# Two chained attentions and a hypernetwork MLP on one core: p loaded once, cast and turned at the start, and a new order of all steps

## The chip, the core and the metric

The kernel runs on one core of one Trainium2 chip. The metric is the device time of one execution in microseconds (us). Times inside the kernel are counted from the first instruction of the profiled execution. Engines are called as in the profile: PE (matmuls; PEld for its weight loads), DVE, ACT, POOL, and SP, which only issues DMAs.

## The reference

The inputs are q, k, v of 8 batches x 8 heads x 576 rows x 64, p of 8 x 8 x 32 x 64, and the matrices moe_w_q and moe_w_k (512 x 64) and moe_w_out (512 x 512), all fp32. The inputs are drawn at random, scaled by 0.1 and 1/sqrt(512).

```python
def sm_attn(qq, kk, vv):
    s = scale * np.matmul(qq, kk.transpose(0, 1, 3, 2))
    a = np.exp(s - np.max(s, axis=-1, keepdims=True))
    a = a / (np.sum(a, axis=-1, keepdims=True) + 1e-09)
    return np.matmul(a, vv)
p_packed = sm_attn(p, k, v)               # 32 rows for each head
x = sm_attn(q, p_packed, p_packed)        # 576 rows, heads side by side: 576 x 512
wq, wk = x @ w_q, x @ w_k                 # 576 x 64
mixed = np.einsum('bst,btd->bsd', scale * np.einsum('bsd,btd->bst', wq, wk), x)
out = np.maximum(mixed, 0.0) @ w_out      # 576 x 512, fp32
```

## The kernel before

The work goes batch by batch through one long sequence of steps; matmuls take bf16 and accumulate in fp32. Steps of neighbouring batches overlap. The order of all steps is written out by hand in one string, ORDER; each word is one step, and the program issues the steps of each engine's queue exactly in the order in which they stand there. The framework adds the waits between the engines. A word reads `NAME.batch.part@engine=banks`: V is DVE, A is ACT, P is POOL, S is SP; a word without an engine is a matmul step on PE, or a DMA; the banks are those of PSUM.

The steps of batch b are, in the order in which data flows:

- LD.k, LD.v, LD.q: the loads of k, v, q, on POOL's queue, cast from fp32 to bf16 by the DMA. Each tensor has four buffers. q0 and q7 come in two halves, LD.r (first half) and LD.q (second half). LD.H and LD.g are the two halves of k of batch 0: H as fp32 by SP, cast by HC on ACT, and g by POOL. Each load on POOL's queue waits, in that queue, for the landing of the eighth load before it.
- KT, QV: turns of k and q on DVE (32 x 32 transposes, L242). PX (one instruction) turns p for batches 2 to 7, EX the part of p for batches 0 and 1.
- S1 (L278 for batches 0 and 1, L288 for the others), X1: the scores of p against k, and their exponentials on ACT. For batches 0 and 1 (DIAG) p stands as block-diagonal copies in the tile pblk, which PB writes (one copy for each of the four quarters of the partitions); for the others the exponentials are turned by TE on DVE.
- PV (L321), RC, PP, PT: the product with v and, by a column of ones in v's tile, the sums; their reciprocal; the scaled p_packed; its turn.
- QK, QKE, QD: p_packed times the two small weights, their copies.
- S2 (L379), X2 (L384), RS (L400), RR (L405), AM (L411), AT (L420, L425), AE: the scores of q, exponentials, sums, reciprocals, the normalized weights (on DVE or POOL), their transposes on PE and the copies out of PSUM. Parts 0, 1, 2 are 256, 256 and 64 (of 128) rows; part 3 is 0 and 1 together, part 4 all.
- WKQ (L447, L452), WE, GM (L473), GE, Y, YE, MX (L498), MR, RL, RLR: the hypernetwork, down to the rectified mixed rows.
- OT (L546; OH for halves), OE, OEF, ST, STF, STH: the output matmul, the copy out of PSUM and the store. HOLD.v7 is a tiny DMA on SP's queue that waits for v of batch 7; the stores behind it on that queue can't start before.
- WARM (L621): matmuls on a tile of zeros whose result nobody reads. WARM.6 has 6 units of 128 columns. They stand where PE's queue is to be kept busy.
- SET: constants (masks, zeros, the column of ones, the identity).

p comes in three ways in the kernel before: E0 and E1, batches 0 and 1 in fp32 by ACT's and SP's queues, cast by EC, turned by EX and copied to pblk by PB; and four casting loads P0 to P3 on POOL's queue, one for each quarter of the partitions, of all batches, turned by PX.

Of the kernel before, what the change touches and what calls it, by code (L numbers as in the profile page):

```python
# [654 lines left out]
```

## Time and profile before

| what | value |
|---|---|
| median of three runs | 106.0 us (105.98 to 106.29) |
| the profiled execution's own time | 105.18 us |
| its span, first to last instruction | 103.3 us |
| granted PE clock, mean over the span | 0.991 |
| PE busy | 96.8 us (94%) |
| DVE, ACT, POOL busy | 75.7, 66.2, 49.9 us |
| moved by DMA | 25.16 MB counted at the landing, mean 244 GB/s |
| read from HBM, written to it | 30.28 MB, 9.44 MB |

Most loads cast fp32 to bf16, so they read twice the bytes that they land; GB/s in the profile counts the landed bytes. A busy PE in the profile includes the WARM steps. A row of the chain gives start, length and what the chain ran through; the chain is the path of work and waits that ended last.

### The profile page before, as it was taken

Reading aid. Unit: us, or ns where it says so; the run is one execution under the profiler, and the core shown is the slowest. Engines: PE = TensorE matmul, PEld = TensorE weight load, DVE = VectorE, ACT = ScalarE, POOL = GpSimd, SP = SyncE. Lnnn points to the kernel's source line nnn. Section 1 sums busy time; section 2 is a strip of 40 time slices with the busy share of each in tenths; the row PEclk is TensorE's granted clock in tenths of the full one; section 3 lists DMA queues with packets and bytes.
Section 4 is the critical chain, followed back from the end, with each engine's and each line's share of the span. In section 5 each row is a group of like instructions: output and inputs, shape, how many; then the busy total and the mean of one; then the engine's idle time right before and its main releaser. Section 6 shows DMA issues by size and latency. Waiting matters only on the chain.

```text
span 103.3 us, 3603 instructions
## 1 busy us (share of the span) xinstructions
PE 96.8 (94%) x1544; PEld 58.4 (57%) x1544; DVE 75.7 (73%) x150; ACT 66.2 (64%) x109; POOL 49.9 (48%) x76
## 2 busy tenths in 40 slices
...
PEclk9999999999999999999999999999999999999996
DMA  2999999999999999999999999999999999999884
GB/s 71 262 149 191 209 208 198 210 211 213 204 213 212 203 208 213 212 206 211 211 210 208 220 208 203 215 211 207 209 259 377 402 410 400 403 409 366 341 305 164
DMA packets 14079, 25.16 MB, mean 244 GB/s; under 512 B 2160, under 2 KB 7024, under 8 KB 14064
## 3 DMA queue, kind: packets, MB, share of 16 engines
...
q1 hardware_dynamic: 3200, 7.87, 19.9%
...
HBM read 30.28 MB, written 9.44 MB: 384 GB/s over the span
## 4 chain that ended last, share of the span: by engine, by line
PE 73%; DVE 9%; DMA 5%; ACT 5%; POOL 3%; issue 2%; DVEq 0%; POOLq 0%; ACTq 0%
PE ps L546 25%; PE ps L621 13%; PE ps L321 6%; DMA k_sb<-in_k_dram 5%; PE ps L379 5%; PE ps L452 4%; PE ps L498 4%; PE ps L425 4%; DVE rs L400 3%; ACT e L384 3%; PE ps L447 3%; PE ps L278 2%; PE ps L473 2%; PE ps L288 2%; PE ps L342 2%; POOL a L411 2%
## 5 line engine op out<-in xcount | busy, mean ns | idle before, releaser
L546 PE MATMUL ps<-wout,relu 128*128 128x512 bf16 x124 | 30.5, 380 | 0.0
L411 POOL TENSOR_TENSOR a<-e,rr 128x1024 bf16<-128x1024 f32 (+2 forms) x13 | 15.6, 1211 | 19.1 <-DVE rr L405 11.0
L621 PE MATMUL ps<-o 128*128 128x128 f32 (+3 forms) x76 | 23.6, 452 | 1.3 <-DVE o L134 1.2
L127 ACT ACTIVATE o<-ps 128x1024 f32<-128x1024 f32 (+2 forms) x17 | 15.0, 888 | 6.9 <-PE ps L546 6.3
L546 PEld LDWEIGHTS <-relu 128*128 128x128 bf16 x124 | 10.7, 98 | 12.3 <-issue 1.8
L621 PEld LDWEIGHTS ps<-o 128*128 128x128 f32 x76 | 12.7, 220 | 7.1 <-issue 4.9
L384 ACT ACTIVATE e<-ps 128x256 f32<-128x256 f32 (+2 forms) x19 | 11.3, 621 | 5.9 <-PE ps L379 5.5
L509 ACT ACTIVATE relu<-ps 128x1024 bf16<-128x1024 f32 (+1 forms) x14 | 12.7, 933 | 2.2 <-PE ps L498 1.1
L242 DVE STREAM_TRANSPOSE kT<-k_sb 128x1152 uint32<-128x1152 uint32 (+1 forms) x9 | 11.1, 1232 | 3.0 <-DMA k_sb<-in_k_dram 2.9
L176 POOL DMA_DIRECT2D v_sb<-in_v_dram x16 | 10.1, 637 | 6.4 <-PE ps L425 2.1
L242 DVE STREAM_TRANSPOSE qT<-q_sb 128x1152 uint32<-128x1152 uint32 (+1 forms) x10 | 11.2, 1119 | 0.7 <-DMA q_sb<-in_q_dram 0.7
L400 DVE TENSOR_REDUCE rs<-e 128x16 f32<-128x512 f32 (+2 forms) x13 | 10.9, 846 | 0.5 <-ACT e L384 0.4
L321 PE MATMUL ps<-v_sb,e 64*64 64x192 bf16 x288 | 7.5, 245 | 0.7 <-DVE o L131 0.7
L299 ACT ACTIVATE e1T<-ps 128x576 bf16<-128x576 f32 x12 | 7.2, 663 | 1.3 <-PE ps L288 1.2
L127 ACT ACTIVATE aT<-ps 128x128 bf16<-128x128 f32 (+2 forms) x11 | 5.3, 506 | 3.6 <-PE ps L425 2.1
L321 PEld LDWEIGHTS <-e 64*64 64x64 bf16 x288 | 6.0, 107 | 2.6 <-issue 0.9
L127 ACT ACTIVATE wkq<-ps 128x448 bf16<-128x448 f32 (+1 forms) x9 | 6.3, 713 | 1.7 <-PE ps L452 1.4
L452 PE MATMUL ps<-aT,pqk 128*128 128x256 bf16 (+1 forms) x48 | 6.8, 246 | 0.1
L379 PEld LDWEIGHTS <-qT 64*128 64x128 bf16 x320 | 5.5, 94 | 2.3 <-issue 0.7
L379 PE MATMUL ps<-ppT,qT 64*128 64x64 bf16 x320 | 6.6, 190 | 0.0
L179 POOL DMA_DIRECT2D k_sb<-in_k_dram x7 | 5.2, 745 | 2.7 <-ACT g L127 2.7
L447 PE MATMUL ps<-pqk,aT 128*128 128x64 bf16 x80 | 6.1, 194 | 0.1
...
## 6 DMA issues: line engine op xcount, KB each, us to landing
...
```

The costliest lines, as they stand in the source:

```text
L127: nc.scalar.activation(o, i, COPY)
L176: nc.gpsimd.dma_start(v_bufs[b % NL][halves(i), 0:7:2], src)
L242: nc.vector.transpose(o, i)
L321: nc.tensor.matmul(T["pv", b][halves(cc), i], lhsT, rhs, start=n == 0, stop=n == R - 1, skip_group_check=True)
L379: nc.tensor.matmul(ps[:, y, t - t0, i], lhsT, rhs, start=e == 0, stop=e == 1)
L384: nc.scalar.activation(e2[:, t0:t1].rearrange("a t (i y n) -> a y (t i) n", i=2, y=2), T["s2", b, c].rearrange("a y t i n -> a y (t i) n") ...
L400: nc.vector.tensor_reduce(rs[:, t0 * H:t1 * H], src, axis=AX, op=ADD)
L411: e.tensor_tensor(a2[:, t0:t1].rearrange("a t i (u l) -> a (t i u) l", l=L), e2v(b, c), T["rr", b][:, t0 * H:t1 * H].to_broadcast((P, (t1 ...
L452: nc.tensor.matmul(o, pqk[:, i, Dl:], aT[:, i, c0:c1], start=i == 0, stop=i == 1)
L509: nc.scalar.activation(o, i, RELU)
L546: nc.tensor.matmul(ps, lhsT, wout[:, j, :], start=j == 0, stop=j == NJ - 1)
L621: nc.tensor.matmul(bank(int(bk), [w]), warm[:, 0:P], rhs, start=True, stop=True)
```

## The change

p is loaded by one DMA on ACT's queue (LD.N), in fp32, for all batches. NC casts it in two halves, one on ACT and one on DVE; PX turns it in two halves on DVE, at the start. PB copies the block-diagonal parts for batches 0 and 1 from the turned p, two on DVE and two on ACT. LD.E0, LD.E1, LD.P0 to LD.P3, EC and EX are gone. The whole ORDER is new, with the same steps of the batches otherwise: 48 steps are on another engine than before (AM of batches 0 and 1, of part 2 of batch 2 and QD of several batches move to POOL; AM.6.3 moves to DVE; the others change mainly between DVE and ACT), the loads stand in another order towards the end (r7 is last, behind two stores on POOL's queue), and the WARM steps after S1.0 have 46 units instead of 62, those before it 21 instead of 20.

```diff
-SET.warm@V SET.v3@V SET.pz0@V LD.E0@A SET.tab@A SET.aT1@V LD.H@S LD.P3 LD.E1@S EC@A EX@V PB.0.1@V LD.g0
-SET.v0@P HC@A PB.0.3@V PB.0.2@V KT.0.0@V KT.0.1@V LD.v0 PB.0.0@P WARM.4=0 WARM.16.128=0 S1.0=0,1,2 X1.0.0@A WARM.6=3
-PV.0.0=4,5 PV.0.1 RC.0@V LD.q0 SET.mask@P SET.idf@V SET.aT0@V QV.0.1@V PP.0.0@V LD.P2 LD.r0 PP.0.1@V PT.0@V
-SET.v2@V LD.W0 QV.0.0@V WARM.15=3 S2.0.2=6,7 LD.k1 LD.W1 SET.aT2@V LD.P1 KT.1.2@V S2.0.1=0,1 X2.0.1@A RS.0.1@V
-SET.v1@P S2.0.0=2,3 X2.0.0@A LD.v1 LD.P0 WARM.8=4 QK.0=4 RR.0.1@V AM.0.1@V QKE.0@A LD.q1 RS.0.0@V SET.aff@P
-SET.idb@V WARM.3=5 S1.1=0,1,2 X1.1.0@A WARM.6=5 PV.1.0=4,5 PV.1.1 X2.0.2@A RR.0.0@V AT.0.1=3 AM.0.0@V AT.0.0=2
-AE.0.0@A RC.1@V PP.1.1@V RS.0.2@V RR.0.2@V AM.0.2@V AE.0.1@A QD.0@A WARM.5=0 WKQ.0.0=0,1 AT.0.2=5 LD.k2
-AE.0.2@A WARM.1=6 WKQ.0.2 LD.v2 WE.0.0@A WKQ.0.1 LD.q2 LD.k3 WE.0.1@A WARM.3=6 GM.0=5 PP.1.0@V PT.1@V QK.1=4
-QV.1.2@V S2.1.1=6,7 GE.0@A S2.1.0=2,3 LD.O PX@V S2.1.2=0,1 KT.2.2@V QKE.1@A X2.1.1@A RS.1.1@V X2.1.0@A Y.0=4,5
-YE.0@A WARM.1=6 S1.2=6,7,2,3 X2.1.2@A LD.v3 RS.1.0@V MX.0.1=4,5 RR.1.1@V X1.2.0@A TE.2.0@V X1.2.1@A TE.2.1@V
-RR.1.0@V WARM.7=0 PV.2.0=0,1 PV.2.1 RL.0.1@A RS.1.2@V AM.1.0@V QD.1@A MR.0=6,7 RLR.0@A LD.k4 RR.1.2@V
-MX.0.0=2,3 LD.q3 RC.2@V AT.1.0=4 AM.1.2@V AT.1.2=5 AE.1.2@A RL.0.0@A PP.2.1@V AM.1.1@P AT.1.1=6 AE.1.1@A
-PP.2.0@V AE.1.0@V WARM.2=7 WKQ.1.0=0,1 WKQ.1.2 WARM.2=7 WKQ.1.1 QV.2.2@V WE.1.0@A PT.2@V S2.2.3=4,5 S2.2.2=2,3
-KT.3.2@V WE.1.1@A GM.1=7 QK.2=6 GE.1@V WARM.3=0 Y.1=0,1 X2.2.2@A QKE.2@V S1.3=2,3,6,7 X2.2.3@A RS.2.4@V
-RR.2.4@V LD.v4 X1.3.1@A TE.3.1@V X1.3.0@A TE.3.0@V OT.0.0=4,5 OT.0.1 LD.q4 YE.1@A AM.2.2@V OT.0.2=6,7 OE.0.0@V
-OT.0.3 MR.1=2,3 OE.0.1@A RLR.1@V MX.1.1=0,1 PV.3.0=4,5 PV.3.1 RL.1.1@A RC.3@V PP.3.1@V PP.3.0@V KT.4.2@V
-AM.2.3@P QD.2@P AT.2.3=2 AE.2.3@A OT.1.4=3 MX.1.0=6,7 AT.2.2=5 OEF.1.4@A AE.2.2@V WKQ.2.0=0,1 PT.3@V QV.3.2@V
...
-PP.5.0@V AM.4.3@P PP.5.1@V RL.3.0@A MX.3.1=4,5 RL.3.1@V LD.k7 QV.5.2@V OT.2.1 OE.2.0@A LD.v7 AT.4.2=2 AE.4.2@A
-AT.4.3=3 AE.4.3@A LD.r7 OT.3.0=0,1 MR.3=4,5 RLR.3@A LD.q7 OT.3.1 KT.6.2@V OE.3.0@A WKQ.4.0=6,7 WKQ.4.1 PT.5@V
-WKQ.4.2 S1.6=2,3,4,5 OT.3.4=0 WE.4.2@V GM.4=1 X1.6.0@A TE.6.0@V S2.5.2=6,7 S2.5.3=2,3 X1.6.1@A TE.6.1@V
-OEF.3.4@V GE.4@A X2.5.2@A HOLD.v7 Y.4=4,5 PV.6.0=6,7 X2.5.3@A ST.1.4 YE.4@V PV.6.1 RC.6@V PP.6.0@V QK.5=1
...
-PV.7.1 QV.7.0@V AM.6.2@P GE.5@A Y.5=4,5 RC.7@V AT.6.2=3 PP.7.0@V ST.1.0 WKQ.6.0=6,7 WKQ.6.1 AE.6.2@A YE.5@A
-PP.7.1@V PT.7@V WKQ.6.2 MR.5=2,3 ST.3.0 MX.5.1=4,5 RLR.5@V WE.6.2@A RL.5.1@V S2.7.0=0,1 X2.7.0@A MX.5.0=2,3
-RL.5.0@A GM.6=6 OT.5.4=7 RS.7.0@V RR.7.0@V GE.6@A S2.7.2=0,1 ST.2.1@P S2.7.1=4,5 X2.7.2@A QK.7=6 AM.7.0@P
-Y.6=2,3 X2.7.1@A OEF.5.4@V RS.7.2@V OT.5.0=0,1 QKE.7@V YE.6@A MX.6.0=4,5 ST.0.1@P MR.6=2,3 MX.6.1=6,7 RR.7.2@V
...
-OEF.6.2@A STF.6.2 MR.7=2,3 RLF.7.0.0@A MX.7.1=4,5 OT.6.3 RLR.7@V OT.7.4=0 RLF.7.1.0@V OEF.6.3@V STF.6.3
-RLF.7.0.1@A OEF.7.4@V ST.7.4 RLF.7.1.1@A OT.7.2=2 OEF.7.2@A STF.7.2 OT.7.1=3 OEF.7.1@A STF.7.1 OT.7.0=6
-OEF.7.0@A STF.7.0 OH.7.1=4 OH.7.0=5 OEH.7.0@A STH.7.0 OEH.7.1@V STH.7.1@A
+LD.H@S SET.warm@V SET.v0@V SET.pz0@V SET.aT1@V LD.N@A SET.tab@A SET.idf@V SET.aT0@V SET.aT2@V LD.g0 NC.1@A
+NC.0@V PX.0@V PX.1@V PB.0.0@V PB.0.1@V HC@A PB.0.2@A PB.0.3@A KT.0.0@V KT.0.1@V LD.v0 LD.r0 LD.q0 LD.k1 LD.W0
+LD.W1 SET.mask@P SET.aff@P SET.v1@P SET.idb@V WARM.4=0 WARM.17.128=0 S1.0=0,1,2 X1.0.0@A WARM.6=3 PV.0.0=4,5
+PV.0.1 RC.0@V PP.0.1@V PP.0.0@V QV.0.0@V PT.0@V QV.0.1@V WARM.12=3 S2.0.2=6,7 X2.0.2@A LD.v1 LD.q1 SET.v2@P
+S2.0.0=0,1 X2.0.0@A RS.0.2@V RR.0.2@V S2.0.1=2,3 X2.0.1@A LD.k2 AM.0.2@P WARM.6=5 AT.0.2=5 RS.0.0@V RR.0.0@V
+WARM.2=4 QK.0=4 AM.0.0@P AE.0.2@A WARM.1=6 AT.0.0=5 QKE.0@A KT.1.2@V LD.v2 AE.0.0@A S1.1=0,1,2 QD.0@P RS.0.1@V
+RR.0.1@V WKQ.0.0=6,7 WKQ.0.2 X1.1.0@A AM.0.1@P WARM.2=3 AT.0.1=3 LD.q2 AE.0.1@V PV.1.0=4,5 LD.k3 PV.1.1 RC.1@V
+PP.1.1@V WKQ.0.1 WE.0.0@A LD.O WE.0.1@A PP.1.0@V WARM.2=0 GM.0=0 GE.0@A WARM.1=1 Y.0=2,3 PT.1@V QK.1=1 YE.0@A
+WARM.1=6 MR.0=4,5 QV.1.2@V S2.1.2=6,7 X2.1.2@A S2.1.1=2,3 QKE.1@V X2.1.1@A RLR.0@V S2.1.0=0,1 SET.v3@P LD.v3
+RS.1.2@V MX.0.0=4,5 RR.1.2@V KT.2.2@V AM.1.2@P MX.0.1=6,7 WARM.3=2 AT.1.2=2 X2.1.0@A RS.1.0@V RR.1.0@V
+RL.0.0@A AE.1.2@A WARM.2=3 S1.2=0,1,4,5 X1.2.1@A AM.1.0@P WARM.7=3 AT.1.0=3 RS.1.1@V X1.2.0@A TE.2.1@V
+RL.0.1@A RR.1.1@V TE.2.0@V PV.2.0=4,5 PV.2.1 AM.1.1@P AT.1.1=2 RC.2@V PP.2.1@V AE.1.0@A QD.1@P WKQ.1.0=0,1
+WKQ.1.2 LD.k4 AE.1.1@A WKQ.1.1 WE.1.0@A PP.2.0@V PT.2@V QK.2=0 WE.1.1@A WARM.1=6 GM.1=6 QKE.2@A QV.2.2@V
+S2.2.2=2,3 X2.2.2@A GE.1@V Y.1=4,5 YE.1@A KT.3.2@V S2.2.3=0,1 X2.2.3@A LD.q3 MR.1=6,7 RLR.1@A MX.1.1=2,3
+RS.2.4@V MX.1.0=4,5 LD.v4 RL.1.1@A S1.3=0,1,6,7 X1.3.1@A QD.2@P X1.3.0@A OT.0.2=2,3 OT.0.3 OE.0.1@A TE.3.1@V
+OT.0.0=6,7 OT.0.1 RR.2.4@V OE.0.0@A RL.1.0@V AM.2.3@P AT.2.3=0 AM.2.2@P AT.2.2=1 TE.3.0@V PV.3.0=4,5 LD.q4
+PV.3.1 AE.2.3@V WKQ.2.0=2,3 RC.3@V PP.3.1@V AE.2.2@A WKQ.2.1 WKQ.2.2 WE.2.2@A LD.k5 PP.3.0@V PT.3@V OT.1.0=6,7
...
+MX.3.0=6,7 RL.3.0@A LD.q7 PP.5.0@V MX.3.1=4,5 RL.3.1@V OT.2.1 KT.6.2@V AT.4.2=1 AE.4.2@A AT.4.3=0 OT.3.0=6,7
+LD.v7 HOLD.v7 OE.2.0@A MR.3=4,5 PT.5@V OT.3.1 AE.4.3@A WKQ.4.0=2,3 QV.5.2@V RLR.3@A OE.3.0@A WKQ.4.1 WKQ.4.2
+WE.4.2@V S1.6=0,1,4,5 X1.6.1@A TE.6.1@V OT.3.4=6 GM.4=7 X1.6.0@A TE.6.0@V S2.5.2=2,3 S2.5.3=4,5 GE.4@A Y.4=0,1
+OEF.3.4@V X2.5.2@A YE.4@V PV.6.0=2,3 ST.1.4@P PV.6.1 X2.5.3@A HA.5@P QK.5=7 QKE.5@A RC.6@V PP.6.0@V ST.1.1@P
+MX.4.1=0,1 LD.r7 MX.4.0=4,5 PP.6.1@V RL.4.1@A PT.6@V MR.4=6,7 QV.6.2@V RLR.4@A RS.5.4@V OT.3.2=2,3 RL.4.0@A
...
+QD.6@P Y.5=4,5 AE.6.2@A WKQ.6.0=0,1 YE.5@A ST.4.1 WKQ.6.1 WKQ.6.2 RC.7@V PP.7.0@V PP.7.1@V MR.5=2,3 RLR.5@A
+PT.7@V WE.6.2@A MX.5.1=4,5 QV.7.0@V ST.3.0 MX.5.0=6,7 RL.5.0@A QK.7=2 RL.5.1@V OT.5.4=3 OEF.5.4@V ST.5.4
+GM.6=0 GE.6@A ST.0.1 QKE.7@V S2.7.2=4,5 S2.7.1=6,7 QD.7@P X2.7.2@A S2.7.0=0,1 X2.7.1@A RS.7.2@V Y.6=4,5 YE.6@A
+RS.7.1@V OT.5.0=2,3 X2.7.0@A MR.6=6,7 RR.7.1@V AM.7.1@P RLR.6@A MX.6.1=4,5 RS.7.0@V RR.7.0@V RL.6.1@A
...
+MX.7.0=2,3 RLF.7.0.0@A ST.6.0 MR.7=4,5 OT.6.3 RLR.7@V OEF.6.3@A RLF.7.1.1@V OT.7.4=6 STF.6.3 RLF.7.0.1@V
+OT.7.2=7 OEF.7.2@A OEF.7.4@V OT.7.0=4 OEF.7.0@V OT.7.1=5 OEF.7.1@A ST.7.4 OH.7.1=0 OEH.7.1@A STF.7.2 STF.7.0
+STF.7.1 STH.7.1@A OH.7.0=2 OEH.7.0@V STH.7.0
@@ -154,14 +154,9 @@
         a, b = x[0], x[1:]
         if a == "g":
             nc.gpsimd.dma_start(k_in[0][:, 1], pairs(k, 0)[:, 1])
-        elif a == "P":
-            c = int(b)
-            src = p.rearrange("b (i c) (y l) d -> c (b i) y (l d)", i=2, y=2)
-            nc.gpsimd.dma_start(pbf[quarter(c)], src[c])
-        elif a == "E":
-            b = int(b)
-            src = p[b].rearrange("(i c) l d -> (c l) i d", i=2)
-            (nc.sync if eng == "S" else nc.scalar).dma_start(p32[:, 2 * b:2 * b + 2], src)
+        elif a == "N":
+            src = p.rearrange("b (i c) (y l) d -> (c y) (b i) (l d)", i=2, y=2)
+            (nc.sync if eng == "S" else nc.scalar).dma_start(p32, src)
         elif a == "W":
             w = (moe_w_k, moe_w_q)[int(b)].rearrange("(i c j e) m -> (c j) i (e m)", i=2, c=4, e=2)
             nc.gpsimd.dma_start(wqk[:, :, int(b)].rearrange("a i e m -> a i (e m)"), w)
@@ -225,12 +220,10 @@
     pbf = T["o"][NO - 4].rearrange("a t n -> a (t n)")[:, 0:L * Dh // 4].bitcast(bf16)
     warm = T["o"][NO - 5].rearrange("a t n -> a (t n)")[:, 0:256]
     spot = T["o"][NO - 5].rearrange("a t n -> a (t n)")[0:32, 1024:1026]
-    p32 = T["o"][NO - 1].rearrange("a t n -> a (t n)")[:, 0:4 * Dh].rearrange("a (u d) -> a u d", u=4)
+    p32 = T["o"][NO - 1].rearrange("a t n -> a (t n)")[:, 0:L * Dh // 2]
     spare = T["o"][NO - 2].rearrange("a t n -> a (t n)")
-    pe = spare[:, 0:4 * L].bitcast(bf16).rearrange("a (u l e) -> a u l e", u=4, l=L)
     pblk = spare[:, 512:512 + 256 * ND].bitcast(bf16).rearrange("a (u c l e) -> a u c l e", c=4, l=L, e=2)
     h32 = T["o"][0].rearrange("a t n -> a (t n)")[:, 0:RQ * Dh]
-    pbe = T["o"][NO - 1].rearrange("a t n -> a (t n)")[:, 4 * Dh:6 * Dh].bitcast(bf16)
 
     def new(key, b, shape, dt=bf16, bufs=NB):
         if key not in T:
@@ -241,22 +234,22 @@
     def blocks(o, i):
         nc.vector.transpose(o, i)
 
-    def EC(eng, bk):
-        copy(eng, pbe, p32.rearrange("a u d -> a (u d)"))
+    def NC(x, eng, bk):
+        n = L * Dh // 4
+        copy(eng, pbf[:, x * n:(x + 1) * n], p32[:, x * n:(x + 1) * n])
 
     def HC(eng, bk):
         copy(eng, k_in[0][:, 0], h32)
 
-    def EX(eng, bk):
-        blocks(pe.rearrange("a u l e -> a (u l e)").bitcast(u32), pbe.bitcast(u32))
-
-    def PX(eng, bk):
-        blocks(pT.rearrange("a u (y l) e -> a (u y l e)", y=2).bitcast(u32).rearrange("a (u l) -> a l u", l=L // 2),
-               pbf.bitcast(u32).rearrange("a (l n) -> a l n", l=L // 2))
+    def PX(x, eng, bk):
+        ls = slice(x * L // 4, (x + 1) * L // 4)
+        blocks(pT.rearrange("a u l e -> a (u l e)").bitcast(u32)
+               .rearrange("a (u y l) -> a l y u", y=2, l=L // 2)[:, ls],
+               pbf.bitcast(u32).rearrange("a (l y u) -> a l y u", l=L // 2, y=2)[:, ls])
 
     def PB(n, c, eng, bk):
         us = slice(0, 2 * ND)
-        copy(eng, pblk[quarter(c), us, c], pe[quarter(c), us])
+        copy(eng, pblk[quarter(c), us, c], pT[quarter(c), us])
 
     def KT(b, x, eng, bk):
         kT = new("kT", b, [P, 2, R, 2 * GQ, 2], bufs=NE)
@@ -595,7 +588,7 @@
         q = nc.scalar if eng == "A" else nc.sync
         q.dma_start(orows(b)[:, :, t * D:(t + 1) * D], T["o", b][:, t])
 
-    steps = dict(EC=EC, HC=HC, EX=EX, PX=PX, PB=PB, KT=KT, S1=S1, X1=X1, TE=TE, PV=PV, RC=RC, PP=PP,
+    steps = dict(NC=NC, HC=HC, PX=PX, PB=PB, KT=KT, S1=S1, X1=X1, TE=TE, PV=PV, RC=RC, PP=PP,
                  PT=PT, QK=QK, QKE=QKE, QD=QD, QV=QV, S2=S2, X2=X2, HA=HA, RS=RS, RR=RR, AM=AM,
                  AT=AT, AE=AE, WKQ=WKQ, WE=WE, GM=GM, GE=GE, Y=Y, YE=YE, MX=MX, MR=MR, RL=RL, RLF=RLF,
                  RLR=RLR, OT=OT, OE=OE, OEF=OEF, ST=ST, STF=STF,
```

29 lines of the change are left out of this document (14 added, 15 removed).

## The prediction

> **What bounds the kernel now.** I read the page first, then stretches of time with the DMA columns, then the chain that ended last in order of time.
>
> ```profile
> PE 96.8 (94%) x1544; PEld 58.4 (57%) x1544; DVE 75.7 (73%) x150; ACT 66.2 (64%) x109; POOL 49.9 (48%) x76
> PEclk9999999999999999999999999999999999999996
> DMA  2999999999999999999999999999999999999884
> L621 PE MATMUL ps<-o 128*128 128x128 f32 (+3 forms) x76 | 23.6, 452 | 1.3 <-DVE o L134 1.2
> ```
>
> PE looks full, but 23.6 us of it are the WARM fillers (L621), which compute nothing. The DMA row is full from the second slice almost to the end. Two resources are near their limits: a DMA stream that never pauses, and a PE queue in fixed order whose early waits are covered by fillers. The stretches give the stream's rates (the columns after each engine's busy time: granted clock, DMA share, GB/s).
>
> ```profile
> 0.00:4.00 4.00, 2.80 (x7) 1.77 (x8) 1.38 (x5) 1.49 (x2) 2.58 (x8) 1.00 0.51 168
> 4.00:8.00 4.00, 4.00 (x29) 3.98 (x28) 2.24 (x6) 1.47 (x2) 2.83 (x10) 1.00 0.99 155
> 12.00:70.00 58.00, 56.64 (x1040) 33.68 (x1038) 49.97 (x98) 39.45 (x65) 29.17 (x41) 1.00 1.15 209
> 90.00:96.00 6.00, 6.00 (x52) 2.76 (x49) 2.76 (x5) 4.48 (x8) 0.00 (x0) 1.00 0.97 387
> ```
>
> Casting loads land 209 GB/s, stores 387. From 4 to 8 us the loads land only 155: the stream has (209-155) x 4 us, 216 KB or 1.0 us, of room there. Now the chain, at the places that the change touches.
>
> ```profile
> 2.03 5.55 DMA k_sb<-in_k_dram
> 8.44 1.23 PE ps L278 x35
> 9.67 1.49 PE ps L621 x4
> 12.02 3.42 PE ps L621 x8
> 15.44 0.71 PE ps L379 x40
> 26.80 0.36 PE ps L473 x10
> 31.53 0.87 PE ps L321 x36
> 43.08 0.94 PE ps L321 x36
> 99.51 0.38 ACT o L127
> ```
>
> S1.0 starts at 8.44 when the second half of k0 is there and turned, S2.0 at 15.44, GM.0 at 26.80, PV.2 at 31.53, PV.3 at 43.08; from there PE is the chain up to 99.51. So whatever the early steps win or lose by PV.3 is carried to the end if PE then keeps its pace.
>
> **The change part by part, on these five landmarks.** The durations (of a line's groups: count, then min/median/max in ns, first and last start, shapes):
>
> ```profile
> 4.90 0.42 ACT L127 ACTIVATE o<-o 128x256 bf16<-128x256 f32 x1 [2.16 <-DMA o<-in_p_dram]
> L127 ACT ACTIVATE k_sb<-o x1: 1147/1147/1147, 5.2 to 5.2; 128x1152 bf16<-128x1152 f32 x1
> L131 DVE COPY orem<-ps x3: 627/652/692, 68.6 to 96.0; 128x512 f32<-128x512 f32 x3
> L131 DVE COPY o<-o x3: 218/218/326, 5.7 to 6.3; 32x256 bf16<-32x256 bf16 x3
> L242 DVE STREAM_TRANSPOSE e<-e1T x12: 422/478/481, 30.3 to 77.9; 128x288 uint32<-128x288 uint32 x12
> L242 DVE STREAM_TRANSPOSE qT<-q_sb x10: 730/1338/1379, 12.4 to 80.1; 128x1152 uint32<-128x1152 uint32 x6, 128x576 uint32<-128x576 uint32 x4
> L242 DVE STREAM_TRANSPOSE pT<-o x1: 1010/1010/1010, 26.3 to 26.3; 128x512 uint32<-128x512 uint32 x1
> L242 DVE STREAM_TRANSPOSE kT<-k_sb x9: 778/1368/1382, 6.5 to 73.3; 128x1152 uint32<-128x1152 uint32 x7, 128x576 uint32<-128x576 uint32 x2
> L384 ACT ACTIVATE e<-ps x19: 378/592/1033, 16.0 to 84.6; 128x256 f32<-128x256 f32 x8, 128x512 f32<-128x512 f32 x6, 128x1024 f32<-128x1024 f32 x5
> L400 DVE TENSOR_REDUCE rs<-e x13: 360/673/1485, 18.9 to 85.6; 128x16 f32<-128x512 f32 x6, 128x40 f32<-128x1280 f32 x4, 128x8 f32<-128x256 f32 x3
> L405 DVE RECIPROCAL rr<-rs x14: 194/253/404, 19.6 to 86.2; 128x16 f32<-128x16 f32 x6, 128x40 f32<-128x40 f32 x5, 128x8 f32<-128x8 f32 x3
> L411 POOL TENSOR_TENSOR a<-e,rr x13: 606/1042/1914, 30.2 to 86.8; 128x1024 bf16<-128x1024 f32 x5, 128x256 bf16<-128x256 f32 x5, 128x512 bf16<-128x512 f32 x3
> L411 DVE TENSOR_TENSOR a<-e,rr x6: 405/684/1732, 19.9 to 40.2; 128x512 bf16<-128x512 f32 x3, 128x256 bf16<-128x256 f32 x3
> ```
>
> *p arrives.* Before, 128 KB (E0, E1) were there when EC began, at 4.90. LD.N brings 512 KB, 393 KB more: 1.0 us at the stores' 387 GB/s, the nearest uncast rate, if nothing overlaps; nothing if it all falls into the 1.0 us of room. I take half: p at 5.4, bounds 4.9 to 5.9.
>
> *S1.0.* All of DVE's new work then stands in a row ahead of it: NC.0 0.65, PX.0 and PX.1 half of 1.01 each, two PB 0.22 each, KT.0.0 and KT.0.1 0.78 each: 3.7 us, so S1.0 starts at 9.1 instead of 8.44 (bounds 8.6 to 9.6). ACT beside it: NC.1 about 0.6 (between 0.42 and 1.15 by width), HC 1.15, ending 7.2 ahead of KT.0.0 at 7.5, and its two PB, at most 0.42 each, end by 8.0. The second half of k0 leads POOL's queue now instead of standing behind P3 (64 KB, 0.3 us), and shares the DMA engines with p; I leave it at 7.6, needed at 8.3. Price of the start: 0.7 us.
>
> *To S2.0.* v0 lands under cover of X1.0. Then WARM.6, PV.0, RC, PP, QV.0 half, PT, QV.0 half and 12 units of WARM instead of 15. A unit costs 0.23 to 0.25 us (3.42/15, 1.49/6), three fewer are 0.7 us, so S2.0 starts at about 15.6 against 15.44. In all, the fillers after S1.0 go from 62 units to 46, 3.7 us; that is no gain by itself: it is cover that must not be missed.
>
> *Batch 0 to GM.0.* Before, X2.0.2 stood behind X1.1 on ACT and all three AM.0 on DVE among KT.1, RS and RR. Now the three X2 follow each other (0.38, 0.59, 0.59) and POOL does the AM. DVE from 16.2: RS 0.41, RR 0.2, RS 0.67, RR 0.25, KT.1.2 1.38, RS 0.67, RR 0.25, ending at 20.0. POOL's queue: k2, AM.0.2, AM.0.0, two v2 loads (their issue waits for landings due by 17.5), QD.0, AM.0.1 (1.04) to 21.7. Then AT, AE, PV.1 0.87, WKQ.0.1 and WE (AE and WE some 0.5 each by the widths above): GM.0 at 23.9, 2.9 us earlier than 26.80.
>
> *Batch 1 to PV.2.* Little of this lasts. QV.1 waits for q1 and DVE; from 24.2: QV 1.35, X2 0.38, RS and RR 0.6, KT.2 1.38 (28.4), RS and RR 0.9, RS 0.67, two TE 0.48 with RR 0.25 between: PV.2 at 31.2 against 31.53.
>
> *Batch 2 to PV.3.* PV.2 0.87, PP and PT about 1.1 to 33.2, QV.2 1.35, KT.3 1.38; X2.2.3 1.03 ends at 36.65, RS 1.48 at 38.2, TE.3.1 behind X1.3.1 to 39.1, RR 0.40, AM.2.3 on POOL 1.91, AM.2.2 on POOL 0.61: 42.05, PV.3 at 42.2 against 43.08. Before, AM.2.2 stood on DVE beside AM.2.3 on POOL and took 1.73 where its shape costs 0.41; that pair is gone. PE meanwhile does OT.0 and then waits about 1 us uncovered. [...] One such pair is new: AM.6.3 on DVE against AM.5.2 or AM.6.2 on POOL, at most 0.6 us, beside PE work of OT.4. By PV.3 the new order has also done three things that the old one did after it:
>
> ```profile
> 44.02 0.55 PE ps L425 x8
> 45.44 0.32 PE ps L498 x2
> 45.76 0.17 PE ps L420 x2
> ```
>
> AT.2.3, MX.1.0 and AT.2.2, 1.0 us. So PE is ahead by 0.9 + 1.0 = 1.9 us.
>
> *The DMA stream.* The three P loads that stood between the others go: 3 x 65.5 KB at 209 GB/s, 0.95 us. At the start N adds 1.35 us (524 KB at 387), E0, E1 and P3 take away 0.35 and 0.3, leaving 0.7, against 1.0 us of room. So loads from v0 on come 0.25 to 0.95 us earlier; I take 0.65. That matters, because loads land just in time in places:
>
> ```profile
> 78.60 0.78 DVE L242 STREAM_TRANSPOSE qT<-q_sb 128x576 uint32<-128x576 uint32 x1 [0.24 <-DMA q_sb<-in_q_dram]
> ```
>
> *The sum.* PE's order alone gives -1.9, the stream alone -0.65; where a step waits for a load the second holds, elsewhere the first, and stores can start only behind the loads. I take the middle, -1.2. The rest is engine swaps of equal size (ACT against DVE, 0.59 against 0.65 for one width), beside PE work. The tail has the same OT, OH and last store of a 128 KB half: 0.
>
> **Rivals.**
> *The stream alone sets the pace* (for it: the wait at 78.60 and the DMA row; against: the last slices of that row are 8, 8, 4, so the end isn't DMA-full): -0.65, 105.35 us.
>
> *Nothing changes:* the shorter fillers only uncover waits and the early gain drains into them, as 2.9 us at GM.0 shrink to 0.3 at PV.2 in my own working: 106.0.
>
> *The half of q7 is late* (slower). LD.r7 now stands behind ST.1.4 and ST.1.1 on POOL's queue, and QV.7.0 on DVE ahead of RL.5.1 and S2.7. The rows of S2.7 before, and of what the new order does before it instead of after (MX.5.0, GM.6, OT.5.4; QK.7 adds some 0.3):
>
> ```profile
> 81.95 0.38 PE ps L379 x16
> 82.33 0.39 PE ps L498 x2
> 82.72 0.40 PE ps L473 x10
> 83.12 0.86 PE ps L546 x4
> ```
>
> That is 1.95 us, so S2.7 is due at 81.95 + 1.95 - 1.2 = 82.7 and r7 by 81.9. v7 lands at about 78.6 - 1.4 - 0.65 = 76.5 (one 288 KB half less); the two stores, 786 KB, take 2.0 us, r7 1.4 alone or 2.8 beside SP's stores: 79.9 to 81.3. It holds by 0.6 us or more. Past 81.9 every us counts in full, and past 83.1 the change loses; if the stores ahead of it are halved as well (2 us more, 83.3) and SP's take a still larger share, r7 lands near 84.5: 107.4.
>
> *p is late* (slower). The chain has k0's second half under way for 5.55 us. If N, too, lands only at 7.5, S1.0 is at 11.2, 2.1 us past my 9.1; if all of it carries, -1.2 becomes +0.9: 106.9.
>
> *The clock falls* (slower). The last digit of PEclk is 6, a mean of 0.6 to 0.7 over 2.58 us: a fall to half would have come 1.5 to 2.1 us before 103.3, so some 2 us after the last matmul. Before, PE's longest uncovered wait was this one:
>
> ```profile
> 43.08 0.94 PE L321 MATMUL ps<-v_sb,e 64*64 64x192 bf16 x36 [0.71 <-DVE o L131]
> ```
>
> I expect 1 us. Should a wait reach 2 us, some 3.4 us at half clock cost 1.7: 107.0 with half of the gain lost. [...]
>
> **How the numbers follow.** The profiled execution took 105.18 us with a span of 103.3; the three runs have a median of 106.0. I apply the difference to the median: 106.0 - 1.2 = 104.8. Chances: forecast 0.45, stream alone 0.17, nothing 0.08, late r7 0.14, late p 0.10, clock 0.06. Faster by over 0.3% (0.3 us, about what a measurement of this kernel can tell) 0.62, the same 0.08, slower 0.30. The low end takes the 1.9 whole with the start's lower bound, another 0.5: 103.6. The high end reaches to the clock case and part of the late r7: 107.1.
>
> **What would show it.** Right: S1.0 near 9.1, GM.0 near 24, PV.3 near 42 with AT.2.3 ahead of it, no P loads, qT's last waits under 0.5 us, PEclk without a gap. Wrong: PV.3 at 43 or later; an idle stretch of PE between 75 and 84 released by q7; S1.0 past 10; fillers gone and PE waits of 1 us or more in their place.

## The result, and the profile after

The changed kernel takes 112.46 us (median of 5 runs, 111.85 to 112.76) against 106.0: slower, ratio 1.058 [1.052, 1.064]. The forecast was 104.8. The profiled execution took 112.67 us, its span is 110.9 us. Where a median and a ratio below disagree, the ratio is the one to read: it leaves out disturbed executions, which the medians hold.

The page of the changed kernel, the lines that answer to those of before:

```profile
PE 96.0 (87%) x1526; PEld 59.9 (54%) x1540; DVE 71.5 (65%) x137; ACT 67.5 (61%) x114; POOL 52.1 (47%) x80
PEclk9999855899999999999999999999999999999999
DMA  3799999998999999999999999999999999707994
```

PE is busy for about as long as before, in a span 7.6 us longer. The clock has a gap in slices 5 to 7. The chain that ended last, at the same places:

```profile
0.74 10.44 DMA o<-in_p_dram
14.72 2.13 PE ps L271 x34
16.85 2.86 PE ps L614 x4
23.50 0.71 PE ps L372 x35
31.82 0.35 PE ps L466 x6
38.69 0.89 PE ps L314 x36
50.20 0.87 PE ps L314 x36
107.00 0.42 DVE o L131
```

The chain now begins with p: issued at 0.74, there at 11.18. S1.0 (L271) starts at 14.72 instead of 8.44, 6.3 us late, and with WARM.6 behind it (L614) it runs at a clock of 0.50: 2.13 and 2.86 us where before had 1.23 and 1.49. By S2.0 (23.50) the kernel is 8.1 us behind; at GM.0 (31.82) 5.0, at PV.2 7.2, at PV.3 7.1, at the last copy 7.5. So the loss arises in the first 23.5 us, and what the steps up to GM.0 win back is gone again by PV.2. The first matmul of S1.0 and the wait ahead of it, and stretches (columns as in the prediction):

```profile
14.06 0.32 PE L271 MATMUL ps<-o,kT 128*64 128x128 bf16 x1 [5.47 <-DVE kT L235]
4.00:8.00 4.00, 4.00 (x28) 4.00 (x28) 0.00 (x0) 0.00 (x0) 3.75 (x11) 1.00 0.89 158
14.00:16.00 2.00, 1.60 (x25) 1.41 (x27) 0.77 (x3) 0.00 (x0) 1.32 (x3) 0.50 1.10 209
```

PE has nothing to do for 5.47 us before S1.0, and the clock is at 0.50 in the stretch from 14 to 16 us. From 4 to 8 us the DMA engines land no more than before (158 GB/s against 155), although p now stands there with 512 KB to bring. The other load that S1.0 needs, the second half of k0, is late as well. POOL issues it at 1.27 us, and the row gives its time to landing:

```profile
k_sb<-in_k_dram POOLq DMA_DIRECT2D x1, 288.0 KB, 10.2
```

It is there at 11.48 instead of 7.59, and only the casts and turns of p ahead of KT.0.1 keep it out of the chain.

### The profile page after: what moved, and what is told of

Read it like the earlier page. It is cut to its first block, busy times and chain, and to the rows that moved or that the text cites. A ratio compares the mean times of both kernels' runs of the same rounds, so it can differ in the third digit from the quotient of the medians.

```text
span 110.9 us, 3579 instructions
## 1 busy us (share of the span) xinstructions
PE 96.0 (87%) x1526; PEld 59.9 (54%) x1540; DVE 71.5 (65%) x137; ACT 67.5 (61%) x114; POOL 52.1 (47%) x80
## 4 chain that ended last, share of the span: by engine, by line
PE 67%; DMA 9%; DVE 9%; ACT 4%; issue 4%; POOL 2%; DVEq 0%; ACTq 0%; POOLq 0%
PE ps L539 24%; PE ps L614 10%; DMA o<-in_p_dram 9%; PE ps L314 6%; PE ps L418 4%; PE ps L372 3%; PE ps L271 3%; PE ps L445 3%; DVE kT L235 2%; PE ps L440 2%; POOL a L404 2%; PE ps L491 2%; PE ps L335 2%; PE ps L466 2%; DVE rs L393 2%
## 5 line engine op out<-in xcount | busy, mean ns | idle before, releaser
L404 POOL TENSOR_TENSOR a<-e,rr 128x256 bf16<-128x256 f32 (+2 forms) x18 | 19.6, 1099 | 26.7 <-DVE rr L398 18.7
L539 PE MATMUL ps<-wout,relu 128*128 128x512 bf16 x113 | 29.0, 380 | 1.2 <-ACT relu L502 0.4
L614 PE MATMUL ps<-o 128*128 128x128 f32 (+3 forms) x72 | 22.0, 449 | 1.2 <-DVE o L134 1.2
L127 ACT ACTIVATE o<-ps 128x1024 f32<-128x1024 f32 (+2 forms) x18 | 16.0, 893 | 6.8 <-PE ps L539 6.5
L614 PEld LDWEIGHTS ps<-o 128*128 128x128 f32 x72 | 12.5, 234 | 6.4 <-issue 4.4
L377 ACT ACTIVATE e<-ps 128x256 f32<-128x256 f32 (+2 forms) x19 | 11.2, 623 | 7.3 <-PE ps L372 6.6
L171 POOL DMA_DIRECT2D v_sb<-in_v_dram x16 | 10.2, 650 | 4.3 <-DMA k_sb<-in_k_dram 3.7
L502 ACT ACTIVATE relu<-ps 128x1024 bf16<-128x1024 f32 (+1 forms) x12 | 11.3, 957 | 0.7 <-PE ps L491 0.7
L235 DVE STREAM_TRANSPOSE kT<-k_sb 128x1152 uint32<-128x1152 uint32 (+1 forms) x9 | 10.9, 1218 | 0.0
L271 PE MATMUL ps<-o,kT 128*64 128x128 bf16 x72 | 3.7, 265 | 5.8 <-DVE kT L235 5.8
L318 DVE RECIPROCAL rec<-ps 128x2 f32<-128x2 f32 x8 | 1.3, 162 | 9.9 <-PE ps L314 9.9
L131 DVE COPY aT<-ps 128x1024 bf16<-128x1024 bf16 (+1 forms) x6 | 3.6, 603 | 5.0 <-PE ps L418 4.8
```

Source lines behind the costliest of these rows:

```text
L127: nc.scalar.activation(o, i, COPY)
L171: nc.gpsimd.dma_start(v_bufs[b % NL][halves(i), 0:7:2], src)
L235: nc.vector.transpose(o, i)
L377: nc.scalar.activation(e2[:, t0:t1].rearrange("a t (i y n) -> a y (t i) n", i=2, y=2), T["s2", b, c].rearrange("a y t i n -> a y (t i) n") ...
L404: e.tensor_tensor(a2[:, t0:t1].rearrange("a t i (u l) -> a (t i u) l", l=L), e2v(b, c), T["rr", b][:, t0 * H:t1 * H].to_broadcast((P, (t1 ...
L502: nc.scalar.activation(o, i, RELU)
```

## The experiments

Each has its time with the kernel before run on the same chip; a ratio is to that. e9, e10, e13, e14 and e18 are one execution each, used for what they show of the arrival.

**Cover, order and path apart (e2, e3, e4).** e2 lengthens the fillers ahead of S1.0; e3 has the new order with the old loads of p (E0, E1, P0 to P3, EC, EX, PX); e4 the old order with the new path of p.

```diff
-WARM.17.128=0            # e2
+WARM.39.128=0
```

> The changed kernel with 43 units of fillers ahead of S1.0 instead of 21, so that PE stays busy until p is turned. If the clock's fall costs what the longer S1.0 (2.13 against 1.23 us), the fillers and PV.0 show: S2.0 starts some 2 us earlier than at 23.4, and the time is 110.3 us. If later steps wait for loads anyway: 112.4 us. If the fillers end late, S1.0 starts later than 14.7.

> The new order with p's old path: E0 and E1 in fp32, four casting loads of p on POOL's queue, EC and EX, the late turn of p. Theory A: S1.0 at 8.5 us, time 104.5 to 106. Theory C (the new order itself loses): 108 us or more.

> The old order with p's new path as the change has it: one DMA on ACT's queue, cast and turned at the start. Theory A: S1.0 at about 14 us, PE idle before it, the clock falls; 111 to 113 us. Theory C: 106 to 107.5 us.

e2: 110.60 us, ratio 1.035 [1.026, 1.045], with a clock of 1.0 in the profiled execution. S1.0 and S2.0 in its chain:

```profile
14.33 1.23 PE ps L271 x35
20.69 0.70 PE ps L372 x32
```

From S1.0 to S2.0 it takes 6.36 us, the changed kernel 8.78. So some 2.4 of the 6.5 us lost are the clock's fall, and the two ratios say the same, give or take 1.2 us. S2.0 starts 2.8 us earlier, as the first case expected. e3: 107.17, 1.011 [1.007, 1.016], between its two theories. e4: 114.62, 1.082 [1.075, 1.088], above both. So the path of p is the loss; the new order with the old loads is no gain either, but 1.1 us slower. Part of that is a place where two things meet that the changed kernel keeps apart. Timeline of e3 around AM.0.2:

```profile
16.47 0.20 DVE L405 RECIPROCAL rr<-rs 128x8 f32<-128x8 f32 x1
17.42 0.72 POOL L179 DMA_DIRECT2D k_sb<-in_k_dram  x1 [2.45 <-DVE rs L400]
18.16 1.63 POOL L411 TENSOR_TENSOR a<-e,rr 128x256 bf16<-128x256 f32 x2
```

AM.0.2 could start at 16.67, but the load of k2 stands ahead of it in POOL's queue, and this load is issued only at 17.42. It waits for the eighth load before it, as v1's first load does in the changed kernel (issued at 12.02, the load of g landed at 11.48); with the loads P0 to P3 in the queue that is k1, which lands at 17.14, without them a half of q0. And e3's one instruction of PX stood in the chain for 1.04 us ahead of KT.2.

**The order repaired (e12).**

```diff
-LD.k2 AM.0.2@P ... RR.1.2@V PX@V KT.2.2@V
+AM.0.2@P LD.k2 ... RR.0.1@V PX@V WKQ.0.0 ... RR.1.2@V KT.2.2@V
```

> The new order with the old loads of p, with two steps moved: AM.0.2 ahead of the load of k2 on GpSimd (it stood behind that issue from 16.7 to 18.2 us) and the transposes of p from 27.9 us, where they stood ahead of S1.2 for 1.0 us, to behind RR.0.1. If the new order is worth what the forecast said and the 1.1 us of the new order with the old loads came from these two places: 104.4 to 105.5. If not: 106.5 to 107.5.

105.66 us over 10 runs against 105.96, ratio 0.998 [0.994, 1.001]. The two places held all of the 1.1 us, but the new order with the old loads is then worth about 0.25 us (between nothing and 0.6, by the interval), not 1.2: neither expectation was met.

**Why p is late: sixteen engines (e1).** p has 128 rows of 4 KB. The changed kernel's access pattern has 8 (c, y) outside, 16 (batch, half) at a pitch of 32 KB inside. e1 brings the same rows in four loads, each with 16 outside.

```diff
-src = p.rearrange("b (i c) (y l) d -> (c y) (b i) (l d)", i=2, y=2)
-nc.scalar.dma_start(p32, src)
+src = p.rearrange("b (i c) (y l) d -> c (b i) y (l d)", i=2, y=2)
+for c in range(4): nc.scalar.dma_start(p32[quarter(c)], src[c])
```

> The changed kernel, but p comes by four DMAs on ACT's queue, one for each quarter of the partitions, with 16 as the outermost count of each instead of 8 in the one DMA. Theory A (the one DMA of p runs on 8 of the 16 engines, comes at 11.1 us and holds up k0 on those engines; the rest follows from that): p is there by 6 us, S1.0 starts at 9 to 9.7, PE has no long idle stretch, the granted clock stays full; 104.8 us if the new order's gain in the middle is as forecast, up to 106.3 if it is none. Theory B (rows of 4 KB that lie 32 KB apart are slow to read on any number of engines): p still after 9 us, 110 us or more. Theory C (the new order itself loses): p early, and still over 108 us.

111.73 us, 1.049 [1.035, 1.063]: p is there 1.0 us earlier, at 10.2, not by 6 as theory A had it. I took that for a proof against the number of engines, and turned to what runs beside p.

**What runs beside p (e5, e6, e9, e11).** In e5 and e6 POOL waits for p after the load of g (the second half of k0), in e9 ahead of it; e6 has the four loads. e11 exchanges the queues of H and p.

```diff
+SET.wait@P     # four 32x1 copies out of p32 to a scratch tile; e5, e6: ahead of LD.v0, e9: ahead of LD.g0
-LD.H@S ... LD.N@A      # e11
+LD.N@S ... LD.H@A
```

> The changed kernel, but GpSimd waits for p (four tiny copies out of the fp32 tile) after the load of the second half of k0 and before the load of v0, so that p shares the DMA engines with H and g alone. Theory D (sharing: the hardware queue gets little once GpSimd's casting loads stand on the same engines): p lands at 7 to 8 us instead of 11.2, by the 130 GB/s of its first stretch, S1.0 starts at 10.5 to 11.5, and the time is 107 to 109.5. Theory A/B (p's own pattern is slow, whatever runs beside it): p still lands at 10 us or later, all loads behind it start 8 us late, and the time is 113 or more.

> The same wait, with p in four loads that use all 16 engines. Theory D: p lands at 5.5 to 6.5 us, S1.0 starts at 9 to 10, and the time is 105.5 to 107.5, the stream of loads losing some 2 us at its beginning. Theory A/B by the pitch of the rows: p lands at 9 us or later, 112 or more.

> The changed kernel with the wait for p put ahead of all of GpSimd's loads: p shares the DMA engines with H alone. Theory E (p is slow of itself, by the order in which its rows are fetched and by its 8 engines): p lands at 7.5 to 8.5 us, little ahead of the 9.1 us that it took beside the second half of k0. Theory D (any casting load beside it slows it): p lands at 5.5 to 6.5 us.

> The changed kernel with the two hardware queues' loads exchanged: p first, by SyncE at 0.6 us, and the first half of k0 by ScalarE. Theory E: p, without a head start of the other load, still takes 5 us or more from its first packet and lands at 7.5 us or later; the first half of k0 comes at about 6. Theory D: p lands at 5 us, since it is through before GpSimd's loads start at 4 us, and the first half of k0 then comes late, at 7 to 8. Time 106.5 to 109 under both, nearer to the lower end under D.

The chains of e5, e9 and e11, and two stretches of e9:

```profile
0.73 8.37 DMA o<-in_p_dram
```
```profile
0.74 7.58 DMA o<-in_p_dram
4.00:7.50 3.50, 3.50 (x21) 3.50 (x21) 0.00 (x0) 0.00 (x0) 0.00 (x0) 1.00 0.47 123
4.00:8.00 4.00, 4.00 (x25) 4.00 (x25) 0.00 (x0) 0.00 (x0) 0.00 (x0) 1.00 0.41 108
```
```profile
0.75 10.11 DMA o<-in_p_dram
```

p takes 10.44 us to arrive beside all of POOL's loads, 8.37 beside g alone, 7.58 beside none of them. So POOL's loads cost 2.9 us, but by itself p is slow as well. The rows of e9 say how: with nothing but p under way, the DMA share of the 16 engines is 0.41, and 0.47 up to 7.5 us, where p's last packet ends. That is what about half of them at work would give. Times: e5 110.44, 1.043 [1.038, 1.048]; e6 110.43, 1.042 [1.035, 1.048]; e9 112.4; e11 112.08, 1.059 [1.054, 1.065]: an earlier place on another queue buys p only 0.3 us. Its first packet starts at 3.42, when H is nearly through (last packet at 4.0). e9 landed p as its theory E said. e6 (9.0 us) and e11 (10.9) landed it as late as A/B and E said, but with other times; e5 (9.1) fell between its two theories. GpSimd's copies in e6 show when the first two of the four loads landed:

```profile
5.11 0.18 POOL L203 CAST touch<-o 32x1 bf16<-32x1 f32 x1 [3.12 <-DMA o<-in_p_dram]
8.50 0.18 POOL L204 CAST touch<-o 32x1 bf16<-32x1 f32 x1 [3.21 <-DMA o<-in_p_dram]
```

The first quarter is there at 5.1, the second 3.4 us later. By the trace's semaphore records, 15 of the second quarter's 16 landings were there at 7.1 and the last came at 8.45. Why four loads are so slow stays open. That e1 spoke against the number of engines in the one load was a wrong reading of it.

**p late, on purpose (e7, e8).** The old early loads E0 and E1 for batches 0 and 1, and the one fp32 load of all p, behind HC in ACT's order, in place of P0 to P3; e7 in the old order, e8 in the new one.

```diff
-LD.P3 ... LD.P2 ... LD.P1 ... LD.P0 ... PX@V
+HC@A LD.N@A ... NC.0@A NC.1@A PX.0@V PX.1@V
```

> The kernel before with its early loads of p for batches 0 and 1 kept, but the one fp32 load of all p (cast by ScalarE, turned by VectorE) issued by ScalarE after the first cast of k, in place of GpSimd's four casting loads; needed only at about 27 us. Theory D: p takes 8 us or more, beside the stream, without anybody waiting; 105.3 to 106.3, since four issues of GpSimd (0.7 us each) go. If the fp32 load slows the stream itself: over 106.5.

> The same with the new order of all steps: S1.0 at 9 us, GpSimd without the four loads of p. Theory of the forecast (the new order is worth some 1.2 us once p is there in time, and the +1.1 us of the new order with the old loads of p came from GpSimd, whose queue held AM.0.2 behind its 8th-last load): 104.3 to 105.5. Rival (the new order is itself slower, whoever loads p): 106.5 to 107.5.

112.23 us, 1.048 [1.041, 1.056], and 110.31, 1.030 [1.022, 1.038]. Both expectations failed: nobody waits for p, and it still costs 3 to 5 us. The chain of e7 has a half of q0 in place of p:

```profile
6.15 10.71 DMA q_sb<-in_q_dram
```

The fp32 load slows the casting loads that run beside it: QV.0.0 starts at 19.04 instead of 14.52 (in a profiled execution of 113.31 us). The semaphore records show that only half of the landings are held up. Of the 16 that make up this half of q0, 8 are there by 12.42, the other 8 come only from 15.46 to 16.87; before, all 16 came from 11.20 to 12.35. The second half of k0 in the changed kernel is split alike: 8 landings by 9.52, 8 from 10.92 to 11.48.

**Rows in the order of memory (e10, e13).** The same 512 KB on the same queue, 128 rows one behind the other; e13 writes them as 8 blocks of 16 adjoining rows. Rows land in other partitions.

```diff
-src = p.rearrange("b (i c) (y l) d -> (c y) (b i) (l d)", i=2, y=2)
+src = p.rearrange("b n (y l) d -> (b n y) (l d)", y=2)                       # e10
+src = bass.AP(p.tensor, p.offset, [[16384, 8], [1024, 16], [1, 1024]])       # e13
```

> The changed kernel with p fetched in the order in which it lies in memory, 128 rows of 4 KB one behind the other, so that rows land in other partitions and the output is another: only the arrival counts. Queue, bytes, packets and everything beside it are as in the changed kernel. Theory E: p lands at 5.5 to 6.5 us, and the time is 105 to 106.5. Theory D: p lands at 9 us or later, over 109.5.

> The changed kernel with p fetched as 8 blocks of 16 rows, each block 64 KB that lie together, so that 8 DMA engines carry it as in the changed kernel, but without its pitch of 32 KB; rows land in other partitions, and only the arrival counts. If the 8 engines are what makes p late: p lands at 8 us or later beside the loads of GpSimd, and the time is 108.5 or more. If the pitch of 32 KB is: p lands at 6.0 to 6.5, 105 to 106.

The chain and a stretch of e10:

```profile
0.75 5.19 DMA o<-in_p_dram
9.49 1.23 PE ps L271 x30
4.00:8.00 4.00, 4.00 (x23) 4.00 (x23) 1.93 (x5) 2.02 (x3) 3.75 (x11) 1.00 1.11 271
```

p is there at 5.9, the stretch lands 271 GB/s instead of 158, and the time is 104.84 us. Everything that differs from the changed kernel is the order of p's rows, and with it the shape of the access pattern. e13 answers nothing by its own question: in the trace's packet records its load ends, as that of e10, with 16 four-byte packets, where the changed kernel's ends with 8; the adjoining blocks seem to have been joined, so it is in effect e10 once more (p there at 6.2, S1.0 at 10.34, 106.03 us). Single executions with what is one and the same load thus differ by over 1 us in time.

**Engines or pitch (e14, e18).** e14 has 16 blocks of 8 rows at a pitch of 64 KB in one load; e18 has 8 blocks of 16 rows that begin 3840 bytes apart, which can't be joined. e14 brings the rows to other partitions, e18 brings other data.

```diff
+src = bass.AP(p.tensor, p.offset, [[1024, 16], [16384, 8], [1, 1024]])       # e14
+src = bass.AP(p.tensor, p.offset, [[16384, 8], [960, 16], [1, 1024]])        # e18
```

> The same with 16 blocks of 8 rows, the rows of a block 64 KB apart, in one load: 16 engines with a wide pitch; only the arrival counts. If the 8 engines are what makes p late: p lands at 6.0 to 6.5 us, 105 to 106. If a wide pitch is: at 8 us or later, 108.5 or more.

> The changed kernel with p fetched as 8 blocks of 16 rows of 4 KB that begin 3840 bytes apart (rows overlap, so they can't be joined; other data, only the arrival counts): 8 engines without the wide pitch. If the 8 engines make p late, together with the casting loads that overtake it from 4.5 us: p lands at 8.5 us or later, and the time is 109 or more. If the pitch of 32 KB does: p lands at 6.5 or before, 105 to 107.

The chains of e14 and of e18:

```profile
0.74 5.79 DMA o<-in_p_dram
```
```profile
0.74 10.30 DMA o<-in_p_dram
```

This settles it for the one load. 8 parts with close rows are as late as the changed kernel (10.30 against 10.44; 112.33 us against 112.46), and 16 parts with a wide pitch are in time (5.79). The pitch is innocent; the 8 is the cause. In the packet records, p ends with 8 four-byte packets in the changed kernel, e9 and e18, and with 16 in e10, e13 and e14. In e14 the second half of k0 is no longer split: its 16 landings come from 6.89 to 7.52. In the changed kernel p has 8 landings, from 9.34 to 11.18 (one more record of its semaphore is at 2.04, just behind its issue), where each of the 69 DMAs of the kernel before has 16. I read the 8 as 8 of the 16 engines; no record names the engine, but the share of 0.47 in e9, the 8 four-byte packets and e18 agree. e14 lost its time elsewhere: 107.06 us, over the 105 to 106 that I had expected. Its PE rows and two stretches:

```profile
9.68 0.25 PE L271 MATMUL ps<-o,kT 128*64 128x128 bf16 x1 [1.89 <-DVE kT L235]
10.00:12.00 2.00, 1.66 (x36) 1.56 (x37) 0.39 (x2) 0.40 (x1) 1.36 (x3) 0.87 1.11 210
12.00:13.00 1.00, 1.00 (x2) 0.34 (x1) 0.00 (x0) 0.73 (x1) 0.73 (x2) 0.50 1.11 210
```

PE had 1.89 us without work, then one matmul, then 0.41 us more without work. At about 11.5, when it had been busy again for 1.2 us, the clock fell to 0.50.

**The path alone, with p in time (e16).** The old order with the load of e10.

> The order of steps before, with p in one fp32 load whose rows are fetched as they lie in memory (rows land in other partitions, only the time counts). If the gain of the run with the rows in order over the kernel before comes from the new path of p alone: 104.6 to 105.3; if it takes the new order: 105.7 to 106.5.

107.86 us, ratio 1.009 [1.005, 1.014]: slower, and by the ratio (106.8) still outside both ranges. In the old order PB.0.0 stands on POOL ahead of the halves of q0 and all later loads, and PB.0.0 now needs p, cast and turned. Timeline of e16:

```profile
7.86 0.44 POOL L129 COPY o<-pT 32x256 bf16<-32x256 bf16 x1 [3.70 <-DVE pT L235]
```

3.70 us without a load being issued; before, this wait was 1.00. In e4 it is 7.93, the likely reason why e4 lost more than the changed kernel. So the new path does not pay in the old order as it stands. The new order has PB.0.0 on DVE; the old order with that one step moved was not run.

**A version that computes all of the reference (e15, e17).** p's rows in the order of memory; PX turns them as they lie, and each pair of batches is then copied from the quarter of the partitions where it lies to the four quarters of its heads: batches 0 and 1 by PB, which copies anyway, the others by 12 new steps PC on DVE behind S1.0. e17 also moves two memsets from POOL to DVE's idle start.

```diff
+def PC(j, c, eng, bk):
+    copy(eng, pT[quarter(c), 4 * j:4 * j + 4], pU[quarter(j), :, c])
+SET.idb@V PC.1.0@V ... PC.3.3@V WARM.4=0
-SET.mask@P SET.aff@P SET.v1@P                    # e17
+SET.aT2@V SET.v1@V SET.mask@V LD.g0 ... SET.aff@P
```

> A version that computes all of the reference: the changed kernel with p fetched in the order in which it lies in memory, turned within the partition quarters as before, and taken from the quarter in which a pair of batches lies into the four quarters of its heads: for batches 0 and 1 by the four copies that fill the blocks anyway, for the others by 12 copies of VectorE (0.22 us each by the row of these copies) between 9.6 and 12.3 us, where VectorE waits for S1.0 and its softmax. By the 104.84 of the run with the rows in order: 104.5 to 105.3 if the 12 copies are hidden; 107 if they stand in the chain.

> The version with the rows in order that computes all of the reference, with the memsets of the mask and of v's second buffer moved from GpSimd, where they ran at 6.5 to 8.5 us beside VectorE's first chain, to VectorE, which has nothing to do between 2.7 us and the arrival of p. Theory (the two copies of the blocks took 0.89 us instead of 0.45 because GpSimd's memsets ran beside them): they take 0.45 again, S1.0 starts at 9.5 to 9.9 instead of 10.33, and the time falls by 0.4 to 104.8 to 105.4. Rival (the copies vary by themselves): S1.0 at 10.2 or later, 105.5 to 105.8.

e15: 105.65 us (12 runs) against 105.82, ratio 0.9955 [0.9923, 0.9988], above the 104.5 to 105.3 expected, with S1.0 at 10.33. e17: 105.42 (12 runs) against 105.74, 0.9936 [0.9900, 0.9972]: faster than the kernel before by some 0.7 us (0.3 to 1.1), and so than the changed one. e17's chain, at the same places as above:

```profile
0.74 5.41 DMA o<-in_p_dram
10.06 1.24 PE ps L274 x32
16.43 0.75 PE ps L375 x35
24.79 0.35 PE ps L469 x6
31.67 0.89 PE ps L317 x36
43.02 0.87 PE ps L317 x36
99.53 0.42 DVE o L131
```

The memsets were only a part of the reason for the late S1.0: it moved from 10.33 to 10.06, between the two expectations, and DVE's two copies of PB took 0.62 us, between the 0.45 of e10 and the 0.89 of e15. The timelines show what took the memset's place. DVE and POOL, in e15 and then in e17:

```profile
7.92 0.89 DVE L131 COPY o<-o 32x256 bf16<-32x256 bf16 x2
7.92 0.58 POOL L204 MEMSET v_sb<- 128x576 uint32 x1
```
```profile
7.92 0.62 DVE L131 COPY o<-o 32x256 bf16<-32x256 bf16 x2
7.87 0.65 POOL L171 DMA_DIRECT2D v_sb<-in_v_dram  x1 [0.95 <-DVE o L236]
```

In e15 the first copy takes 0.66 us and ends 0.08 us behind the memset. In e17 POOL, without the memset, issues its next load earlier; the second copy takes 0.39 us and ends 0.02 us behind that issue. The other copy of each pair takes 0.22. In all the traces of this case, each of DVE's copies of this shape that takes more than 0.25 us (19 of them, 0.26 to 0.71 us) ends in this way, within 0.1 us behind a memset, a copy or a DMA issue of POOL. No run tests it by itself.

## Why the prediction was wrong, step by step

*p arrives* failed, and with it the sign. I gave it 5.4 us, between 4.9 and 5.9, by adding 393 KB at the stores' 387 GB/s. That rate is one of stores with 16 landings each, at a DMA share of 0.97; p as written lands in 8 parts, at a share of 0.47 with nothing beside it (e9), and POOL's casting loads beside it make its 7.58 us 10.44. I read that as 8 engines, which p and those loads share. Measured 11.2. The second half of k0, which I left at 7.6, landed at 11.48, its later 8 landings 1.4 us or more behind the others. The bounds were bounds of how much overlaps, not of how fast the load goes, so the true value lay far outside. The rows of before could not have warned me, since every DMA there has 16 landings; a run with nothing beside this load, as e9, would have.

*The rivals.* *p is late* was the right mechanism (chance 0.10) with too small a size: I let p be late by as much as k0's second half, 2.1 us, for 106.9; it was 5.8 us later than forecast. *The clock falls* came on top of it, as its consequence, not beside it: 5.47 us without work, some 2.4 us lost against the 1.7 of that rival. The profile has the clock at 0.50 from 13.2 to 20.0 us, 6.8 us instead of the 3.4 that I had put there. No row of before shows that length, but e5 and e14 do: the mean clocks of e5 are 0.91, 0.50 and 0.73 from 12 to 14, 16 and 18 us, those of e14 0.87 from 10 to 12 us and 0.50, 0.50 and 0.55 in the three us behind, 3.4 us at 0.50 in both. I had put the fall behind a wait of 2 us; in e14 it came though the longest wait was 1.89 us (and 0.41 behind one matmul), in a single execution. In e15 waits of 1.34 and 0.42 left the clock at 1.0. *The half of q7 is late* did not happen: no wait of DVE for it is in the traces of the changed kernel and of e17.

*From S1.0 to PV.3* the lengths held. In e17, with p in time, S1.0 to S2.0 took 6.4 us (forecast 6.5), to GM.0 8.4 (8.3), to PV.2 6.9 (7.3), to PV.3 11.4 (11.0). The last path was another than forecast: PE did not wait 1 us ahead of PV.3, since OT.0 began only at 38.81, behind RL.1, and filled the time to 42.42. That the sum still agreed is in part luck. *S1.0* itself came at 10.06 instead of 9.1: p at 6.15 instead of 5.4, the row of DVE's work 3.9 us instead of 3.7.

*1.0 us of PE's work done ahead* did not become time. The stretch from PV.3 to the last copy, in before and in e17:

```profile
43.08:99.51 56.43, 56.09 (x970) 32.79 (x969) 44.89 (x84) 44.90 (x71) 24.74 (x31) 1.00 1.08 280
```
```profile
43.02:99.53 56.51, 55.47 (x959) 32.67 (x958) 44.56 (x76) 44.47 (x75) 25.11 (x33) 1.00 1.04 271
```

Before, PE waited 0.34 us in all of this stretch; in e17 PE works 0.6 us less and waits 1.04. The work done ahead was swapped for waits: three of 0.38, 0.27 and 0.17 us stand ahead of PV.4, S1.5 and an MX, which wait for DVE. Other traces agree: by their chains the stretch takes 56.8 us in e4 (old order), 56.5 in e10, 56.8 in e12 and in the changed kernel. I had taken PE to keep its pace there, and named nothing that would be late next. Where the 0.7 us of e17 lie, the two traces don't show: up to the last copy they differ by 0.02 us, and that of before is of an execution of 105.18 us, faster than any other of this kernel on record (105.37 at the least). So with p in time the new order brought 0.7 of the 1.2 us forecast, from steps that stay open.

*The DMA stream* was not borne out as a term of its own. No DMA stands in the chain of e17 behind p's arrival, and the new order without P loads (e17) gains 0.64% where the one with them (e12) gains 0.24%, with intervals that overlap; no run here separates the stream. The new pair AM.6.3 on DVE beside AM.6.2 on POOL cost what the prediction feared, and a little more (1.0 us against at most 0.6): in the changed kernel AM.6.2 took 1.58 us, where another AM of its shape took 0.61 (at 82.72), beside PE work:

```profile
84.66 1.23 DVE L404 TENSOR_TENSOR a<-e,rr 128x1024 bf16<-128x1024 f32 x1
84.77 1.58 POOL L404 TENSOR_TENSOR a<-e,rr 128x256 bf16<-128x256 f32 x1 [0.84 <-ACT pqk L127]
```
